# Seven arms by the token count, in steps of 16 rows, for the first products of the experts' second parts

## The chip, the cores and the metric

The kernel runs on one core of a Trainium2 chip. The metric is the device time of one execution in microseconds (us); for the kernel before, the median of three runs is 886.41 us.

## The reference

The reference chains three layers over 3072 tokens of 384 features: a gated linear attention, a mixture of eight experts in which every token goes to two, and a last feed-forward layer. The middle one is where the change lies:

```python
for e in range(E):
    for k in range(2):
        mask = top2[:, k] == e
        if not mask.any():
            continue
        h = np.maximum(x[mask] @ w1[e], 0.0)
        out[mask] += top2_w[mask, k, None] * (h @ w2[e])
```

`w1[e]` is 384 x 1024 and `w2[e]` 1024 x 384. How many tokens an expert gets follows from the inputs. Worked out from the reference's own inputs, the experts 0 to 7 get 766, 738, 811, 777, 800, 755, 719 and 778.

## The kernel before

The attention runs first, in 24 chunks of 128 tokens, and writes each token's features to two of 6656 slots: each of the eight experts (`NE`) owns 832 (`CAP`). [...] The first block holds 320, 384 or 512 slots and is always full; the second one holds the rest (512 for expert 0, 448 for experts 1 and 7, 320 for the others) and is only filled as far as the expert has tokens. Below, this block is called the expert's second part.

A step (`products`, one per block and per `f`, the eight groups of 128 hidden units) has two halves. The first products (`first_products`, line 218) are nine matmuls: weights split into two f16 parts times the tokens of the block, in three pieces of 128 features; their column count is the number of slots taken. The second products (`second_products`, line 237, and `tail_products`, line 269) take the hidden units of the step two steps back (`LAG`) and multiply them with `w2`, 128 slots at a time. `relu` (lines 244 and 252) runs between them on ACT and DVE, over the block's full width whatever the count.

`take_rows` loads the eight counts into registers of PE. For a second part, `either` (line 326) emits a binary tree of compares on the count: each leaf, called an arm here, is the same piece of code for one `cut`, the number of empty slots at the block's end that it leaves out. An arm of the first products is nine pairs of LDWEIGHTS and MATMUL and a jump to the end of the tree (the last arm needs no jump). The tail of the second products has a tree of its own. Before the change both trees use `CUTS` in steps of 32, four arms, or three where an expert's limit is 64. All arms stand in PE's program one behind the other, and the compares jump over those that aren't taken.

The order of the blocks is 0 to 2 with their first parts, then their second parts, then experts 3, 4 and 5 with both parts each, and at the end first parts of 6 and 7 and second parts of 6 and 7. One step of an expert's second part in the middle of its run is, in PE's program: a tree of the first products, three matmuls of the second products (nine for expert 0), and a tree of the tail, in whose arms three more matmuls and the tail's products stand. Second parts thus run, in the profile, for expert 0 near 187 to 217 us, 1 to 244 us, 2 to 268 us, 3 to 317 us, 4 to 367 us, 5 to 412 us and 6 and 7 to 506 us. The last feed-forward layer follows, without any branch on PE, and ends the kernel.

Of the kernel before, what the change touches and what calls it, by code (L numbers as in the profile page):

```python
# [30 lines left out]
def blocks(e):  # L31
    cut = {0: 320, 1: 384, NE - 1: 384}.get(e, 512)
    return (0, cut), (cut, CAP - cut)
# [4 lines left out]
CLEARED = 16  # L38
TAIL = 64
CUTS = (0, 32, 64, 96)  # L40


def parts(e, blk):
    n = blocks(e)[blk][1]
    return [(c, min(128, n - c)) for c in range(0, n, 128)]
# [32 lines left out]
def fast(ctx, tc, flag, f_cols, kq_cols, v_rows, gates, blank, void, w12, w_in, w_out, out):  # L78
# [126 lines left out]
    def lasting(e, blk, name, tag):  # L205
        if order.index((e, blk)) < 2:
            return bank(name, tag)
        if tag not in FIXED:
            FIXED[tag] = bank(name, tag)
        return FIXED[tag]  # L210

    def first_products(ph, n, lhs, key):
        x = XT[key]
        o = 0
        for a in range(3):
            wh, wl = lhs(a)
            for l, r in ((wh, a), (wh, 3 + a), (wl, a)):
                nc.tensor.matmul(ph[:, :n], l, x[:, r, :n], start=(o == 0), stop=(o == 8))  # L218
                o += 1

    def begin_second(key, f, parts):
        if f == 0:
            for i in range(len(parts)):
                new = bank if key[0] == "m" else partial(lasting, *key)
                PY[key, i] = new(f"py{i}", ("b0", "b1", "b5" if len(parts) == 3 else "b2", "b5")[i])[:, :DM]
        return HS.pop((key, f))

    def second_products(hs, key, f, last, rhs, parts):
        wh, wl = (w.rearrange("p a b -> p (a b)") for w in rhs)
        for i, (c0, m) in parts:  # L230
            p = PY[key, i]
            if m == 64:
                ops = [(hs[:, c0:c0 + 2 * m], w) for w in (wh, wl)]
            else:
                ops = [(hs[:, s + c0:s + c0 + m], w) for s, w in ((0, wh), (0, wl), (512, wh))]
            for o, (l, r) in enumerate(ops):
                nc.tensor.matmul(p[:max(m, 128)], l, r, start=(f == 0 and o == 0),  # L237
                                 stop=(f == last and o == len(ops) - 1))
# [17 lines left out]
    def tail_products(hs, e, f, rhs, cut):  # L256
        i, (c0, n) = list(enumerate(parts(e, 1)))[-1]
        p = PY[(e, 1), i].rearrange("p (a r) -> p a r", a=3)
        r = n - cut
        for a in range(3):  # L260
            wh, wl = (w[:, a, :] for w in rhs)
            if n == TAIL:
                both_halves = hs[:, c0:c0 + 2 * n].rearrange("p (h r) -> p h r", h=2)[:, :, :r]
                ops = [(p[:, a].rearrange("p (h r) -> p h r", h=2)[:, :, :r], wh, both_halves),
                       (p[:, a, :r], wl, hs[:, c0:c0 + r])]
            else:
                ops = [(p[:, a, :r], w, hs[:, at:at + r]) for w, at in ((wh, c0), (wl, c0), (wh, 512 + c0))]
            for o, (out_, l, x) in enumerate(ops):
                nc.tensor.matmul(out_, l, x, start=(f == 0 and a == 0 and o == 0),  # L269
                                 stop=(f == 7 and a == 2 and o == len(ops) - 1))  # L270
# [3 lines left out]
    def turn_tail(new):  # L274
        while turns:
            e, i, n, t = turns.pop(0)
            del PY[(e, 1), i]
            p = new("ph", next(tags["ph"]))[:, :DM]
            y = gath.tile([128, DM], F32, name="yo")
            if n == TAIL:  # L280
                nc.tensor.transpose(p[:, :128], t[:, :2 * n], ident)
                nc.tensor.transpose(p[:n, 128:256], t[:, 2 * n:3 * n], ident)
                nc.scalar.activation(y[:n, 128:256], p[n:2 * n, :128], AF.Copy)
                nc.vector.tensor_copy(y[:n].rearrange("p (a r) -> p a r", a=3)[:, 0:3:2],
                                      p[:n, :256].rearrange("p (a r) -> p a r", a=2))
            else:
                for a in range(3):
                    nc.tensor.transpose(p[:n, a * 128:(a + 1) * 128], t[:, a * n:(a + 1) * n], ident)
                nc.vector.tensor_copy(y[:n], p[:n])
            at = (e + 1) * CAP - n  # L290
            stores.append((y_rows[at:at + n, :], y[:n]))

    def results(e, blk):
        for i, (c, n) in enumerate(parts(e, blk)):
            p = PY[(e, blk), i]
            if blk and c + n == blocks(e)[1][1]:
                t = gath.tile([128, DM], F32, name="yo")
                if n == TAIL:
                    packed = t[:, :3 * n].rearrange("p (a r) -> p a r", a=3)
                    p = p.rearrange("p (a r) -> p a r", a=3)  # L300
                    nc.scalar.activation(packed, p[:, :, n:], AF.Copy)
                    nc.vector.tensor_tensor(packed, packed, p[:, :, :n], op=OP.add)
                else:
                    nc.scalar.activation(t, p, AF.Copy)
                turns.append((e, i, n, t))
                continue
            y = gath.tile([128, DM], F32, name="yo")
            PY.pop(((e, blk), i))
            if n == 64:
                nc.scalar.activation(y[:n], p[n:2 * n], AF.Copy)  # L310
                nc.vector.tensor_tensor(y[:n], y[:n], p[:n], op=OP.add)
            elif i % 2:
                nc.vector.tensor_copy(y[:n], p[:n])
            else:
                nc.scalar.activation(y[:n], p[:n], AF.Copy)  # L315
            at = e * CAP + blocks(e)[blk][0] + c
            stores.append((y_rows[at:at + n, :], y[:n]))
# [8 lines left out]
    def either(e, emit, cuts):  # L326
        if e is None or len(cuts) == 1:
            emit(cuts[0])
            return
        half = len(cuts) // 2  # L330
        with tc.If(many[e] > CAP - cuts[half]) as cond:
            either(e, emit, cuts[:half])
        with cond.Else():
            either(e, emit, cuts[half:])

    def products(first, second):
        if first:
            e, blk, f = first
            ph = lasting(e, blk, "ph", next(tags["ph"]))

            def emit_first(cut):
                w = RING[e, f]
                first_products(ph, blocks(e)[blk][1] - cut, lambda a: (w[:, 0, a, :], w[:, 1, a, :]), (e, blk))

        if second:
            e2, blk2, f2 = second
            hs = begin_second((e2, blk2), f2, parts(e2, blk2))

            w2 = RING[e2, f2]
            done = list(enumerate(parts(e2, blk2)))  # L350
            rhs = w2[:, 0, 3:6, :], w2[:, 1, 3:6, :]

            def emit_second(parts):
                second_products(hs, (e2, blk2), f2, 7, rhs, parts)

            def emit_tail(cut):
                emit_second(done[-2:-1])
                if cut < done[-1][1][1]:
                    tail_products(hs, e2, f2, rhs, cut)

        if first:
            either(e if blk else None, emit_first, CUTS[:3] if e in (1, 2) else CUTS)
        turn_tail(partial(lasting, NE - 1, 1))
        if second:
            if blk2:
                emit_second(done[:-2])
                either(e2, emit_tail, CUTS if done[-1][1][1] > TAIL else CUTS[:3])
            else:
                emit_second(done)
        if second and f2 == 7:  # L370
            results(e2, blk2)
        if first:
            relu(*first, ph)

    def moe_first(e, blk, f):
        products((e, blk, f), None)

    def moe_second(e, blk, f):
        products(None, (e, blk, f))
# [12 lines left out]
    def moe_products(n):  # L392
        products(moe_steps[n] if n < len(moe_steps) else None, moe_steps[n - LAG] if n >= LAG else None)
# [558 lines left out]
    for n in range(4, len(moe_steps) + LAG):  # L952
# [8 lines left out]
        e, blk, f = moe_steps[n]  # L961
# [143 lines left out]
    for n in range(M + FF_LAG):  # L1105
        if n < M:
            blk, f = steps[n]
# [317 lines left out]
```

## Time and profile before

| | |
|---|---|
| median of 3 runs | 886.41 us (886.34 to 888.34) |
| the profiled execution, own time | 889.56 us |
| its span | 887.8 us |
| PE busy with matmuls | 873.6 us, 98% |
| ACT / DVE / POOL busy | 600.6 / 575.0 / 172.3 us |
| chain that ended last | PE 91%, DMA 4%, the rest 1% each or less |
| PE's granted clock, mean over the span | 0.999 of full speed |

The span is the time from the first to the last instruction; 1.76 us of the profiled execution lie around it. Busy time of PE is a union of matmuls whose ends are modelled, so the pace of PE is read from the starts of groups that follow each other. PEq and PEld in the views are PE's sequencer, which reads the program, jumps, waits for semaphores and hands matmuls on, and its weight loads. A jump of either kind, with a condition or without, is a COMPARE_BRANCH of line 331 in the profile. Queue q8, "instruction", moves pieces of PE's program.

### The profile page before, as it was taken

How to read it: one execution, taken by the hardware profiler on the slowest of the kernel's cores; microseconds unless marked ns; L12 is line 12 of the kernel's file. 1: busy time of each engine (PE TensorE's matmuls, PEld its weight loads, DVE VectorE, ACT ScalarE, POOL GpSimd, SP SyncE). 2: the span in 40 equal slices, each digit the busy share in tenths (PEclk: the TensorE clock that was granted, in tenths of full speed). 3: DMA queues.
4: the chain of work that ended last, by engine and by line, in shares of the span. 5: the costliest groups of instructions: out<-in, count | busy, mean ns of one | idle time of the engine just before them, and what ended most of it. 6: DMA issues, size and time to landing. Idle time of an engine off the chain costs nothing.

```text
span 887.8 us, 18080 instructions
## 1 busy us (share of the span) xinstructions
PE 873.6 (98%) x6573; PEld 527.8 (59%) x6573; DVE 575.0 (65%) x1174; ACT 600.6 (68%) x1569; POOL 172.3 (19%) x240
## 2 busy tenths in 40 slices
PE   8999999999999999999999999999999999999996
PEld 7888766556665656566566555555555555555553
DVE  7998966733586565767658775565565565565664
ACT  7988855646786566778659776666657656656653
POOL 3488834100000000000004040130220320410000
PEclk9999999999999999999999999999999999999999
DMA  9989999844585665949366531030230220320101
GB/s 254 212 248 282 269 281 274 268 118 98 162 249 172 166 198 112 232 112 220 101 159 174 140 83 29 28 98 18 63 72 10 73 62 10 92 51 1 37 1 40
DMA packets 112343, 116.99 MB, mean 132 GB/s; under 512 B 68208, under 2 KB 91376, under 8 KB 112080
## 3 DMA queue, kind: packets, MB, share of 16 engines
q1 hardware_dynamic: 105792, 96.11, 41.5%
q0 software_dynamic: 6144, 18.88, 6.9%
q8 instruction: 77, 1.26, 0.6%
q14 instruction: 42, 0.34, 0.1%
q10 hardware_dynamic: 288, 0.39, 0.1%
HBM read 72.88 MB, written 30.38 MB: 116 GB/s over the span
## 4 chain that ended last, share of the span: by engine, by line
PE 91%; DMA 4%; POOL 1%; issue 1%; DVE 1%; ACT 1%; SPq 0%; POOLq 0%; DVEq 0%
PE ph L218 42%; PE py L237 41%; DMA kq<-in_kq_cols 2%; PE pY L562 2%; PE pA L539 1%; DMA raw<-in_w 1%; PE py L269 1%; PE pY L554 1%; DMA xt<-xs 1%; PE pkr L578 1%; PE pX L605 1%; DMA v<-in_v_rows 1%; POOL kqT L523 1%; POOL xs L707 1%; PE pt L625 0%
## 5 line engine op out<-in xcount | busy, mean ns | idle before, releaser
L237 PE MATMUL py<-wsplit,hs 128*128 128x384 f16 x2296 | 409.3, 326 | 0.0
L237 PEld LDWEIGHTS <-hs 128*128 128x128 f16 x2296 | 224.4, 98 | 157.7
L218 PE MATMUL ph<-xt,wsplit 128*128 128x512 f16 (+7 forms) x1152 | 211.9, 329 | 2.1 <-DMA xt<-xs 2.1
L218 PE MATMUL ph<-xt,winS 128*128 128x512 f16 x864 | 201.8, 379 | 0.0
L917 DVE SCALAR_TENSOR_TENSOR s<-s,z 128x512 f32<-128x512 f32 x96 | 66.5, 692 | 135.6 <-ACT s L914 135.6
L218 PEld LDWEIGHTS <-wsplit 128*128 128x128 f16 x1152 | 109.5, 98 | 75.0 <-issue 2.8
L913 ACT ACTIVATE z<-ph 128x512 f32<-128x512 f32 x96 | 57.3, 597 | 126.3 <-PE ph L218 126.3
L218 PEld LDWEIGHTS <-winS 128*128 128x128 f16 x864 | 84.4, 98 | 91.5
L252 DVE SCALAR_TENSOR_TENSOR hs<-ph,hs 128x256 f16<-128x256 f32 (+2 forms) x192 | 79.4, 441 | 75.4 <-ACT hs L244 73.2
L244 ACT ACTIVATE hs<-ph 128x512 f16<-128x512 f32 (+3 forms) x128 | 65.7, 513 | 72.7 <-PE ph L218 69.7
L159 DVE SCALAR_TENSOR_TENSOR wsplit<-raw,wsplit 128x768 f16<-128x768 f32 x72 | 68.8, 956 | 26.3 <-ACT wsplit L158 24.5
L164 ACT ACTIVATE junk<-wsplit 128x384 f16<-128x384 f16 x144 | 74.2, 516 | 1.5
L914 ACT ACTIVATE s<-z,bias_a 128x512 f32<-128x512 f32 x96 | 69.3, 722 | 3.1
L919 DVE SCALAR_TENSOR_TENSOR g<-s,ph 128x512 f32<-128x512 f32 x96 | 66.0, 687 | 6.1
L158 ACT ACTIVATE wsplit<-raw 128x768 f16<-128x768 f32 x72 | 60.1, 835 | 13.7 <-DMA raw<-in_w 10.9
L382 POOL CAST spacer<-hs 1x1 f32<-1x1 f16 x22 | 5.8, 262 | 327.5 <-ACT hs L244 326.9
L926 DVE TENSOR_TENSOR hs<-g,hs 128x512 f16<-128x512 f32 x96 | 65.7, 685 | 0.1
L382 POOL COPY spacer<-g 1x1 f32<-1x1 f32 x40 | 19.9, 497 | 215.7 <-DVE g L919 198.8
L925 ACT ACTIVATE hs<-g 128x512 f16<-128x512 f32 x96 | 58.8, 613 | 1.1 <-DVE g L919 1.1
L884 POOL DMA_INDIRECT g<-y_rows,yslot x48 | 50.9, 1061 | 20.9 <-issue 9.9
L707 POOL DMA_INDIRECT xs<-xkeep,yslot x48 | 49.1, 1023 | 15.7 <-issue 9.2
L315 ACT ACTIVATE yo<-py 128x384 f32<-128x384 f32 x26 | 12.8, 491 | 33.0 <-PE py L237 32.2
(163 smaller groups left out, 889.4 us busy)
## 6 DMA issues: line engine op xcount, KB each, us to landing
raw<-in_w SPq DMA_DIRECT2D x64, 384.0 KB
y_rows<-yo SPq DMA_DIRECT2D x48, 192.0 KB
kq<-in_kq_cols SPq DMA_DIRECT2D x42, 192.0 KB
w<-in_moe_w_out SPq DMA_DIRECT2D x32, 192.0 KB
w<-in_moe_w_in SPq DMA_DIRECT2D x24, 256.0 KB
v<-in_v_rows SPq DMA_DIRECT2D x24, 192.0 KB
out<-o SPq DMA_DIRECT2D x22, 192.0 KB
f<-in_f_cols SPq DMA_DIRECT2D x40, 96.0 KB
```

The source lines that it names most:

```text
L158: nc.scalar.activation(t[:, 0], raw, AF.Copy, scale=SW)
L159: nc.vector.scalar_tensor_tensor(t[:, 1], raw, SW, t[:, 0], op0=OP.mult, op1=OP.subtract)
L164: nc.scalar.activation(junk[:, :DM], RING[e, f][:, 0, 3 * i:3 * i + 3, :].rearrange("p a b -> p (a b)"), AF.Square, accum_out=wsum[:, 8 * ...
L218: nc.tensor.matmul(ph[:, :n], l, x[:, r, :n], start=(o == 0), stop=(o == 8))
L237: nc.tensor.matmul(p[:max(m, 128)], l, r, start=(f == 0 and o == 0), stop=(f == last and o == len(ops) - 1))
L244: nc.scalar.activation(hs[:, :n], ph[:, :n], AF.Relu, accum_out=hacc[:, at:at + 1])
L252: nc.vector.scalar_tensor_tensor(hs[:, at:at + hi - lo], ph[:, lo:hi], 0.0, hs[:, lo:hi], op0=OP.max, op1=OP.subtract)
L914: nc.scalar.activation(s, z, AF.Square, scale=1.0 / SZ, bias=bias_a)
L917: nc.vector.scalar_tensor_tensor(s, s, ZD, z, op0=OP.add, op1=OP.mult)
L919: nc.vector.scalar_tensor_tensor(g, s, 0.5, ph, op0=OP.mult, op1=OP.mult)
L925: nc.scalar.activation(hs[:, :512], g, AF.Copy)
L926: nc.vector.tensor_tensor(hs[:, 512:], g, hs[:, :512], op=OP.subtract)
```

## The change

A tuple of cuts in steps of 16 rows takes the place of `CUTS` in the tree of the first products alone: seven arms instead of four, and five instead of three for experts 1 and 2. The tree of the tail stays as it was.

```diff
 TAIL = 64
 CUTS = (0, 32, 64, 96)
+FINE = tuple(range(0, 97, 16))
...
         if first:
-            either(e if blk else None, emit_first, CUTS[:3] if e in (1, 2) else CUTS)
+            either(e if blk else None, emit_first, FINE[:5] if e in (1, 2) else FINE)
```

Two places in PE's program. The first is a step of expert 5's second part (`wsplit` are the weights, `xt` the tokens, `ph` the result; x2 marks two compares that follow each other). Before, from the tree's entry to the second products behind it:

```order
L331 COMPARE_AND_BRANCH x2
...
L218 MATMUL ph<-xt,wsplit 128x320
...
L218 MATMUL ph<-xt,wsplit 128x288
...
L331 COMPARE_AND_BRANCH
...
L218 MATMUL ph<-xt,wsplit 128x256
...
L218 MATMUL ph<-xt,wsplit 128x224
...
L237 LDWEIGHTS hs
```

and with the change, whose lines are one further down:

```order
L332 COMPARE_AND_BRANCH x2
...
L219 MATMUL ph<-xt,wsplit 128x320
...
L332 COMPARE_AND_BRANCH
...
L219 MATMUL ph<-xt,wsplit 128x304
...
L219 MATMUL ph<-xt,wsplit 128x288
...
L332 COMPARE_AND_BRANCH x2
...
L219 MATMUL ph<-xt,wsplit 128x272
...
L219 MATMUL ph<-xt,wsplit 128x256
...
L332 COMPARE_AND_BRANCH
...
L219 MATMUL ph<-xt,wsplit 128x240
...
L219 MATMUL ph<-xt,wsplit 128x224
...
L238 LDWEIGHTS hs
```

Three arms, of 304, 272 and 240 columns, and three compares are new; what comes behind the tree has moved 60 instructions further from its entry. The second place is a step of expert 2's second part. Before:

```order
L331 COMPARE_AND_BRANCH
L218 LDWEIGHTS wsplit
L218 MATMUL ph<-xt,wsplit 128x320
...
L331 UNCONDITIONAL_BRANCH
L331 COMPARE_AND_BRANCH
L218 LDWEIGHTS wsplit
L218 MATMUL ph<-xt,wsplit 128x288
```

and with the change:

```order
L332 COMPARE_AND_BRANCH x2
L219 LDWEIGHTS wsplit
L219 MATMUL ph<-xt,wsplit 128x320
...
L332 UNCONDITIONAL_BRANCH
L219 LDWEIGHTS wsplit
L219 MATMUL ph<-xt,wsplit 128x304
...
L332 UNCONDITIONAL_BRANCH
L332 COMPARE_AND_BRANCH
L219 LDWEIGHTS wsplit
L219 MATMUL ph<-xt,wsplit 128x288
```

A second compare stands at the entry and an arm of 304 columns has come in; further down one of 272 has too. On the other engines the instructions and their order are the same.

## Rows read from the trace of the kernel before

**Rows 1.** The page: span, PE's busy time, the queue of PE's program (packets, MB).

```profile
span 887.8 us, 18080 instructions
...
PE 873.6 (98%) x6573; PEld 527.8 (59%) x6573; DVE 575.0 (65%) x1174; ACT 600.6 (68%) x1569; POOL 172.3 (19%) x240
...
q8 instruction: 77, 1.26, 0.6%
```

**Rows 2.** Busy time by stretch (us; x instructions), PE's granted clock, in 395 to 410.

```profile
395.00:410.00 15.00, 15.00 (x109) 10.52 (x108) 11.83 (x36) 12.72 (x46) 0.00 (x0) 1.00 0.98 224
```

**Rows 3.** Groups of PE by shape, expert 7's: busy, mean ns | idle before.

```profile
L218 PE MATMUL ph<-xt,wsplit 128*128 128x416 f16 x72 | 14.0, 338 | 0.0
```

**Rows 4.** Timeline of PE (start us, us) in second parts of experts 0, 3, 5, 6, 7.

```profile
200.36 1.87 PE L218 MATMUL ph<-xt,wsplit 128*128 128x448 f16 x9
...
203.78 1.87 PE L218 MATMUL ph<-xt,wsplit 128*128 128x448 f16 x9
...
302.74 1.26 PE L218 MATMUL ph<-xt,wsplit 128*128 128x288 f16 x9
...
304.98 1.26 PE L218 MATMUL ph<-xt,wsplit 128*128 128x288 f16 x9
...
404.41 1.15 PE L218 MATMUL ph<-xt,wsplit 128*128 128x256 f16 x9
405.39 1.14 PE L237 MATMUL py<-wsplit,hs 128*128 128x384 f16 x6
406.37 1.15 PE L218 MATMUL ph<-xt,wsplit 128*128 128x256 f16 x9
407.35 1.14 PE L237 MATMUL py<-wsplit,hs 128*128 128x384 f16 x6
...
468.59 1.03 PE L218 MATMUL ph<-xt,wsplit 128*128 128x224 f16 x9
...
470.43 1.03 PE L218 MATMUL ph<-xt,wsplit 128*128 128x224 f16 x9
...
486.59 1.74 PE L218 MATMUL ph<-xt,wsplit 128*128 128x416 f16 x9
488.17 1.63 PE L237 MATMUL py<-wsplit,hs 128*128 128x384 f16 x9
...
489.80 1.74 PE L218 MATMUL ph<-xt,wsplit 128*128 128x416 f16 x9
```

**Rows 5.** All jumps of line 331: ns min/median/max, first and last start us.

```profile
L331 PEldq COMPARE_BRANCH  x328: 70/208/1868, 186.4 to 504.7; - x164
```

**Rows 6.** Six single long jumps of line 331, each in a window around its start.

```profile
L331 PEldq COMPARE_BRANCH  x1: 420/420/420, 401.5 to 401.5; - x1
L331 PEldq COMPARE_BRANCH  x1: 1868/1868/1868, 405.4 to 405.4; - x1
L331 PEldq COMPARE_BRANCH  x1: 417/417/417, 470.5 to 470.5; - x1
L331 PEldq COMPARE_BRANCH  x1: 630/630/630, 474.0 to 474.0; - x1
L331 PEldq COMPARE_BRANCH  x1: 348/348/348, 478.9 to 478.9; - x1
L331 PEldq COMPARE_BRANCH  x1: 1074/1074/1074, 481.4 to 481.4; - x1
```

**Rows 7.** Queue q8 in 403.20:403.30, 479.95:480.05, 470:484 (packets started, MB, share).

```profile
q8 instruction: 1, 0.02, 164.6%
q8 instruction: 1, 0.02, 68.2%
q8 instruction: 4, 0.07, 2.0%
```

**Rows 8.** Queue q8 in 565:590; busy by stretch between its two starts there.

```profile
q8 instruction: 2, 0.03, 0.6%
565.80:589.34 23.54, 23.54 (x129) 12.44 (x128) 14.36 (x23) 14.46 (x32) 9.40 (x12) 1.00 0.30 84
```

## The prediction

> **What bounds the kernel now.** The page comes first: PE is busy for 873.6 of 887.8 us [rows 1]. The timeline of PE then shows how tight that is: in second parts each group starts as the one before ends, and in 395 to 410 us PE is busy for 15.00 of 15.00 us at full granted clock [rows 2, 4]. So a column less on PE is time gained, and a gap on PE is time lost; nothing behind can make up for either, since the last layer is as full (23.54 of 23.54 us) [rows 8]. The third view is that of the sequencer's jumps, and the fourth the queue that brings PE's program. They show what keeps PE fed, and there I find the larger term.
>
> **What the change saves.** The arms follow from the counts. Expert 2 has 811 tokens, 21 slots empty: its cut goes from 0 to 16. Expert 3 (777, 55 empty) and expert 7 (778, 54 empty) go from 32 to 48. Expert 0 (66 empty), 4 (32), 5 (77) and 6 (113) stay at 64, 32, 64 and 96, and expert 1 (94) at its limit of 64. The trace bears the counts out where it can: expert 7 runs 72 matmuls of 416 columns [rows 3]. Nine products of 416 columns take 488.17 - 486.59 = 1.58 us, nine of 256 take 405.39 - 404.41 = 0.98 us [rows 4]: 3.75 ns a column. 16 columns over 8 steps are 0.48 us an expert, for three experts **1.44 us**, all on PE's path. `relu` works on the full width as before.
>
> **What it adds: compares.** Each of the 64 second-part steps runs one compare more. A jump takes 208 ns in the median and 70 at least [rows 5], so 64 cost the sequencer at most some 13 us, 0.2 us a step. I cost them at nothing by themselves: the 328 jumps of before leave PE without a gap, because the sequencer hands matmuls on well ahead. How far ahead can be read at expert 5. The jump that begins at 405.4 [rows 6] belongs to the tree of the tail, between the third and the fourth of the six second products that start at 407.35 [rows 4]; the fourth is due at 407.35 + 0.49 = 407.84. So the sequencer had 2.4 us in hand. That is the cover, and it is gone once the sequencer is late by more.
>
> **What it adds: code.** In the middle steps of experts 3 to 6 PE's program holds 78 instructions for the first products (four arms of 18, three jumps, three compares), 6 for three second products and 46 for the tail's tree, 130 in all. Three more arms with a jump each (57) and three compares make it 190. Counted alike, expert 0 goes from 192 to 252 a step, 7 from 136 to 196, 1 from 116 to 156 and 2 from 110 to 150. This program comes in pieces: 77 packets of 16.4 KB [rows 1], and from one start to the next PE runs 129 + 128 = 257 instructions where nothing is jumped over [rows 8]. Code that is jumped over is brought too: 4 packets start in 470 to 484 us [rows 7], some 1,000 instructions for about eight steps, of which some 35 each are run.
>
> **Is a piece ever late?** Yes, already now. A fetch started at 403.2 to 403.3 and took 164.6% x 16 x 0.1 us = 2.63 us, so it landed by 405.9 [rows 7]; the jump that began at 405.4 lasted 1.87 us and ended at 407.3 [rows 6], 1.4 us after the landing. The fetch of 480.0 took 1.09 us and landed at 481.1; the jump of 481.4 ended at 482.5, again 1.4 us later. Both waited for the newest piece, so only about one piece is brought ahead. The price of a piece is then the time from the end of one such jump to the end of the next. In experts 6 and 7 these ends are 470.9, 474.6, 479.2 and 482.5 [rows 6]: periods of 3.7, 4.6 and 3.3 us, mean **3.87 us**. Before, a piece of expert 6 holds 257/130 = 2.0 steps of 1.84 us (468.59 to 470.43 [rows 4]), 3.6 us of work: supply and demand just meet, and the 2.4 us in hand absorb the rest.
>
> **The sum.** With the change a piece holds less work: for expert 0, with steps of 3.42 us, 3.42 x 257/252 = 3.49 us; for 3 and 4 (2.24 us) 3.03; for 5 (1.96 us) 2.65; for 6 (1.84 us) 2.49; for 7 (3.21 us) 4.21 [rows 4]. Expert 4 runs the same shapes as 3. Experts 1 and 2 have more columns than 3, hence longer steps, and 156 and 150 instructions: at least 2.24 x 257/156 = 3.69, about even. Every piece that holds less than 3.87 us of work puts the sequencer back by the difference. Eight steps of 190 instructions are 5.9 pieces, six borders; the piece behind the first border was brought in the quiet steps before, so I count five waits, and seven for expert 0. Each second part starts with the 2.4 us in hand. PE then stands still for
>
> - expert 0: 7 x 0.38 - 2.4 = 0.3 us
> - experts 3 and 4: 5 x 0.84 - 2.4 = 1.8 us each
> - expert 5: 5 x 1.22 - 2.4 = 3.7 us
> - expert 6: 5 x 1.38 - 2.4 = 4.5 us
>
> together 12.1 us. Less 1.44 us that is **+10.7 us**. The profiled execution took 889.56 us (887.8 of span and 1.76 around it) and would take 900.3; it lies 3.15 us above the median of the runs, so I put the sum on the median: 886.41 + 10.7 = **897.1 us**.
>
> The unknown price is that of a piece, and both bounds come from the same rows. With the shortest period, 3.3 us, only experts 5 and 6 lose, 0.9 + 1.7 us: +1.1 us, 887.5. With the period of expert 5 as a fourth one, from the end of the jump of 401.5 (401.9) to that of 405.4 (407.3), 5.4 us, the mean is 4.25: experts 0, 3, 4, 5 and 6 lose 2.9, 3.7, 3.7, 5.6 and 6.4 us, +20.9, 907.3. I take the mean of the three since expert 6, where they lie, carries most of the loss; the 5.4 holds one fetch of 2.63 us, in a stretch with the DMA engines 98% busy [rows 2].
>
> [...] The rows show waits that end 1.4 us after the newest fetch has landed [rows 6, 7]. [...]
>
> **The rivals.**
>
> - *Not slower: the pieces come faster when they are asked for faster.* The period of 3.87 us is near the 3.6 us that PE's own pace demanded there, so part of it may be demand and not supply. Then the 2.4 us hold: expert 6 stays hidden with a period under 2.49 + 2.4/5 = 2.97 us, which is the point that decides. Only the gain is left: 885.0 us, within 0.3%. Against it: 1.4 us from landing to going on, 1.1 us of transfer (2.0% x 16 x 14 us over four [rows 7]), and a new fetch begins only after the last wait, which already is 2.5 us before any queueing of the fetch. Chance 0.12. [...]
> - *Hardly slower: the short period rules.* 3.3 us each time, 887.5 us, below what a measurement tells apart. For it: one of three periods; against it: the two others and expert 5's. Chance 0.10.
> - *Much slower: the fetch queues behind the weight loads.* As in 5.4 us above, in more than one piece in four: beyond 907 us. For it the 2.63 us of that fetch, against it the 1.1 us mean of four others. Chance 0.10.
> - *The finer arms aren't taken.* The counts are of the reference's own inputs, and the six other block widths fit them; the most that could be missing is the 1.44 us. It only shifts the others.
>
> **How the numbers follow.** The forecast, pieces of 3.4 to 4.25 us, gets 0.68, and its time is 897.1 us. The range reaches from the short period to the long mean, 887 to 907 us: it leaves out the first rival and what lies beyond 907, about 0.2. A measurement of this kernel tells about 0.3% from no change, 2.7 us, that is 883.8 to 889.1. Slower by more: forecast and third rival, 0.78. Within: the first two rivals, 0.20. Faster by more would need twice the gain that the columns hold: 0.02.
>
> **What the profile after would show.** 72 matmuls each of 304, 272 and 400 columns in place of 72 of 320, 288 and 416; nine of 400 columns in 1.52 us. 392 jumps instead of 328, and some 91 packets on q8 (48 x 60 + 16 x 40 = 3,520 more instructions are 13.7 pieces). Jumps over 1 us not twice but at most borders in experts 3 to 6, about 4 us apart; and gaps of about 1 us on PE there that no semaphore ends, before lines 219 and 238. The last layer keeps its length. Wrong it would be if PE stays without gaps in experts 5 and 6, or if gaps come that another engine ends.

## The result, and the profile after

The changed kernel takes 899.0 us in the median of six runs (896.98 to 904.54); six runs of the kernel before give 888.0 us. The ratio is 1.0133, with a 95% interval of 1.0110 to 1.0157: some 11.8 us slower, where 10.7 us (1.012) were forecast. The profiled execution took 896.98 us, the lowest of the six.

Its page, in the lines that answer to [rows 1], and PE's costliest group with its idle time:

```profile
span 895.2 us, 18144 instructions
...
PE 875.1 (98%) x6573; PEld 527.2 (59%) x6573; DVE 576.0 (64%) x1174; ACT 599.9 (67%) x1569; POOL 171.9 (19%) x240
...
q8 instruction: 91, 1.49, 0.7%
...
L219 PE MATMUL ph<-xt,wsplit 128*128 128x512 f16 (+9 forms) x1152 | 211.3, 329 | 7.0 <-issue 5.4
```

The same group before:

```profile
L218 PE MATMUL ph<-xt,wsplit 128*128 128x512 f16 (+7 forms) x1152 | 211.9, 329 | 2.1 <-DMA xt<-xs 2.1
```

The same 6573 matmuls run, 14 more packets come on q8, and PE has begun to wait in its first products for "issue", that is for nothing that the profile shows. The jumps, to be read against [rows 5]:

```profile
L332 PEldq COMPARE_BRANCH  x392: 65/208/2962, 183.5 to 512.9; - x196
```

There are 64 more, as many as there are steps, and the longest has gone from 1.87 to 2.96 us. Sixteen of them last over 1 us, where three did before: the two that the prediction names and a third one at 361.7 us, of 1.10 us. The forms of the first products show that the change does what it says:

```profile
L219 PE MATMUL ph<-xt,wsplit 128*128 128x400 f16 x72 | 13.5, 332 | 0.0
...
L219 PE MATMUL ph<-xt,wsplit 128*128 128x304 f16 x72 | 10.6, 293 | 0.2 <-issue 0.2
...
L219 PE MATMUL ph<-xt,wsplit 128*128 128x272 f16 x72 | 9.6, 279 | 0.8 <-issue 0.8
```

Where the time went is read by stretch: each second part from its first product to that of the next block. The columns are length, then PE's busy time and count, PEld, DVE, ACT, POOL, granted clock, DMA share and GB/s. Before, experts 2 to 7 and the sum of all eight stretches were

```profile
241.70:262.20 20.50, 20.50 (x165) 13.98 (x163) 16.62 (x44) 17.59 (x56) 0.00 (x0) 1.00 0.91 250
292.20:311.70 19.50, 19.50 (x169) 13.83 (x168) 11.04 (x35) 11.87 (x45) 0.00 (x0) 1.00 0.64 171
341.40:361.00 19.60, 19.60 (x171) 13.89 (x169) 11.73 (x36) 12.33 (x46) 0.00 (x0) 1.00 0.67 171
390.70:408.30 17.60, 17.60 (x134) 12.92 (x132) 13.21 (x38) 13.71 (x50) 0.00 (x0) 1.00 0.70 175
462.10:477.80 15.70, 15.70 (x129) 12.20 (x127) 11.17 (x34) 11.91 (x44) 4.17 (x8) 1.00 0.61 140
477.80:505.90 28.10, 28.06 (x208) 16.72 (x207) 23.49 (x54) 23.02 (x62) 5.68 (x9) 1.00 0.64 160
sum 173.10, PE 173.06 PEld 114.77 DVE 109.77 ACT 126.10 POOL 9.85; mean PE 21.63 PEld 14.35 DVE 13.72 ACT 15.76 POOL 1.23
```

and after:

```profile
238.80:260.90 22.10, 20.60 (x167) 13.98 (x165) 17.06 (x44) 18.54 (x57) 0.00 (x0) 1.00 1.06 253
290.80:311.20 20.40, 19.57 (x170) 13.92 (x169) 11.06 (x35) 11.90 (x45) 0.00 (x0) 1.00 0.76 178
340.90:360.60 19.70, 19.70 (x169) 13.90 (x167) 11.68 (x36) 12.27 (x46) 0.00 (x0) 1.00 0.67 135
390.40:412.10 21.70, 19.55 (x134) 13.42 (x133) 13.32 (x38) 13.70 (x50) 0.00 (x0) 0.92 0.83 197
465.90:484.80 18.90, 16.35 (x128) 11.83 (x126) 12.35 (x37) 13.17 (x48) 4.88 (x9) 1.00 0.56 137
484.80:513.50 28.70, 27.70 (x209) 16.72 (x207) 22.30 (x51) 21.68 (x57) 5.02 (x8) 1.00 0.63 145
sum 183.60, PE 175.56 PEld 114.97 DVE 110.28 ACT 126.91 POOL 9.90; mean PE 21.95 PEld 14.37 DVE 13.78 ACT 15.86 POOL 1.24
```

The second parts have grown by 183.60 - 173.10 = 10.5 us; PE, busy for all of them before, now stands still for 183.60 - 175.56 = 8.0 us there. The two profiled executions differ by 7.4 us only, because what lies ahead (the attention and the first parts of experts 0 to 2) happened to end 2.9 us earlier in the later one (the first product of expert 0's second part starts at 186.7 instead of 189.6 us); the last layer took 381.7 us instead of 381.9.

The longest wait, in expert 5, in the timeline of PE:

```profile
402.21 1.16 PE L219 MATMUL ph<-xt,wsplit 128*128 128x256 f16 x9
403.20 1.14 PE L238 MATMUL py<-wsplit,hs 128*128 128x384 f16 x6
406.49 1.55 PE L219 MATMUL ph<-xt,wsplit 128*128 128x256 f16 x9 [2.15 <-issue]
407.83 2.13 PE L238 MATMUL py<-wsplit,hs 128*128 128x384 f16 x6
409.75 1.53 PE L219 MATMUL ph<-xt,wsplit 128*128 128x256 f16 x9
411.12 1.14 PE L238 MATMUL py<-wsplit,hs 128*128 128x384 f16 x6
```

The single jump in it, and the fetch of q8 that starts in 403.75 to 403.85:

```profile
L332 PEldq COMPARE_BRANCH  x1: 2962/2962/2962, 403.5 to 403.5; - x1
```

```profile
q8 instruction: 1, 0.02, 81.2%
```

The fetch took 81.2% x 16 x 0.1 = 1.30 us and landed at 405.1. The jump, begun at 403.5, ended at 406.4, 1.4 us after the landing, and the matmuls start at 406.49. It is the same wait as the 1.87 us of [rows 6], but now the matmuls in hand had run out at 404.3. All sixteen jumps over 1 us end so, 1.2 to 1.5 us after the newest fetch on q8 has landed.

### The profile page after: what moved, and what is told of

The parts are those of the page before. It is cut to its first block, busy times and chain, and to the rows that moved or that the text cites. A ratio compares the mean times of both kernels' runs of the same rounds, so it can differ in the third digit from the quotient of the medians.

```text
span 895.2 us, 18144 instructions
## 1 busy us (share of the span) xinstructions
PE 875.1 (98%) x6573; PEld 527.2 (59%) x6573; DVE 576.0 (64%) x1174; ACT 599.9 (67%) x1569; POOL 171.9 (19%) x240
## 5 line engine op out<-in xcount | busy, mean ns | idle before, releaser
L219 PE MATMUL ph<-xt,wsplit 128*128 128x512 f16 (+9 forms) x1152 | 211.3, 329 | 7.0 <-issue 5.4
```

## The experiments

Theory A is that of the prediction: pieces of PE's program come too late for code that is longer but holds no more work. Theory B is that the compares themselves cost the time. Each ratio is to runs of the kernel before that were taken together with the experiment: 889.11 us in the median for the first four experiments, 887.18 us for the last four.

**The code alone.** An arm that no expert takes (for expert 2 another one than for the rest) gets a tree and copies of its own; cuts and compares on the path stay as before. In the diffs `blk` is 0 for an expert's first part and 1 for its second.

```diff
+            spare = 2 if e == 2 else 0
+            more = range(3 if e in (1, 2) else 4)
+
+            def emit_padded(i):
+                cut = CUTS[i // 32]
+                if blk and cut == CUTS[spare]:
+                    either(e, lambda _: emit_first(cut), [CAP - 5000 - c for c in more])
+                else:
+                    emit_first(cut)
...
-            either(e if blk else None, emit_first, CUTS[:3] if e in (1, 2) else CUTS)
+            either(e if blk else None, emit_padded, CUTS[:3] if e in (1, 2) else CUTS)
```

> The kernel before, with the added code but neither the finer cuts nor a compare more on the path: in one arm that no expert takes (cut 0; for expert 2, which takes that one, cut 64) stand four copies of the arm behind a tree of its own (three copies for experts 1 and 2). Theory A (pieces of PE's program come too late): some 91 packets on q8, 328 jumps run, no column fewer, and PE stands still in second parts of experts 3 to 6 as forecast for the change, 12.1 us: 1.0136 times the kernel before, no less than 1.008. Theory B (the added compares cost the time, the code does not): the time of before, 0.997 to 1.003.

Measured: 1.0175 (1.0157 to 1.0193), 904.18 us against 889.11. Its jumps, its q8 and the sum of its eight second parts:

```profile
L331 PEldq COMPARE_BRANCH  x328: 70/197/2842, 184.5 to 514.6; - x164
```

```profile
q8 instruction: 91, 1.49, 0.7%
```

```profile
sum 185.50, PE 175.25 PEld 114.30 DVE 113.20 ACT 128.09 POOL 9.81; mean PE 21.91 PEld 14.29 DVE 14.15 ACT 16.01 POOL 1.23
```

Code that never runs makes the kernel slower, with no compare more on the path: B falls. It costs 15.6 us by the ratio, against 13.2 of the change with its gain of 1.44 added back, though the intervals of the two overlap; the forecast of 1.0136 (12.1 us) lies below this one. The second parts grew by 185.50 - 173.10 = 12.4 us in the profile, which is the fastest of the five runs (899.79 us). All 13 jumps over 1 us in it end 1.4 to 1.6 us after the newest fetch has landed.

**A compare alone.** One compare more on the path of each step, over two instructions and a jump.

```diff
+            def tree():
+                either(e if blk else None, emit_first, CUTS[:3] if e in (1, 2) else CUTS)
+
+            if blk:
+                with tc.If(many[e] > 5000) as cond:
+                    w = RING[e, f]
+                    nc.tensor.matmul(ph[:, :64], w[:, 0, 0, :], XT[e, blk][:, 0, :64], start=True, stop=True)
+                with cond.Else():
+                    tree()
+            else:
+                tree()
...
-            either(e if blk else None, emit_first, CUTS[:3] if e in (1, 2) else CUTS)
```

> The kernel before with one compare more on the path of each of the 64 second-part steps, and hardly more code: ahead of the tree of the first products stands a compare that never holds, over one LDWEIGHTS, one MATMUL and a jump (four instructions a step). Theory A: 392 jumps are run as in the changed kernel, but a piece still holds 257/134 x 1.84 = 3.5 us of work in expert 6, five waits of 0.3 us stay within the 2.4 us in hand, and the time is that of before, 0.997 to 1.003. Theory B (the compares): 64 x 0.2 us, up to 13 us, 1.012 to 1.015.

Measured: 1.0018 (1.0005 to 1.0032). Inside A's range and far from the 1.012 of B. In its profile the second parts sum to 173.4 us, where 173.1 stood before. The small rest (1.6 us) fits the four instructions a step and the 0.2 us less in hand, but no run parts the two.

**Seven arms for experts 5 and 6 alone.**

```diff
-            either(e if blk else None, emit_first, FINE[:5] if e in (1, 2) else FINE)
+            either(e if blk else None, emit_first, FINE if e in (5, 6) else CUTS[:3] if e in (1, 2) else CUTS)
```

> The seven arms for experts 5 and 6 alone, which take no other cut by them; the others keep four or three. Theory A: 3.7 + 4.5 = 8.2 us slower, 1.009 (1.005 to 1.014), with all long waits in these two second parts. Theory B: 16 of the 64 compares, a quarter of the 12 us: 3 us, 1.0035.

Measured: 1.0096 (1.0070 to 1.0123). B's 1.0035 is excluded. Two of eight experts, those with the shortest steps and no column to gain, cost 8.5 us, about two thirds of the 13.2 us (11.8 and the 1.44) that the change costs before its gain. In its profile the second parts of 5 and 6 last 24.0 and 19.4 us instead of 17.6 and 15.7, while those of 3 and 4 keep 19.6 each, and all five jumps over 1 us stand in 5 and 6.

**Finer arms for experts 2 and 7 alone.**

```diff
-            either(e if blk else None, emit_first, FINE[:5] if e in (1, 2) else FINE)
+            either(e if blk else None, emit_first, FINE if e == 7 else FINE[:5] if e == 2 else CUTS[:3] if e == 1 else CUTS)
```

> The finer arms for experts 2 (five) and 7 (seven) alone; both take a cut of 16 rows more and their steps are long, so that a piece holds about 3.9 and 4.2 us of work. Theory A: the gain without the loss, 2 x 0.48 = 0.96 us faster, 0.999 (0.996 to 1.002), no wait that reaches PE. Theory B: 16 compares, 3 us less 0.96: 1.002 or more.

Measured: 1.0013 (1.0002 to 1.0024), inside A's range, but the gain of 0.96 us isn't there, and B's 1.002 lies inside the interval too: this run doesn't part the two. In its profile these second parts hold two gaps, together more than the 0.96. One of 0.57 us in expert 2 is put down to the weights' split on DVE, which ended 0.2 us before PE went on; it also ended 1.3 us after a fetch had landed (at 259.7 us), so late code is neither shown nor excluded there. The other, 0.55 us in expert 7, is put down to the `yo` of DVE, and nearly the same (0.53 us) stands in the kernel with the columns alone below, which adds no code. What took the gain stays open.

**Six arms**, as a dose between four and seven.

```diff
-            either(e if blk else None, emit_first, CUTS[:3] if e in (1, 2) else CUTS)
+            either(e if blk else None, emit_first, CUTS[:3] if e in (1, 2) else (0, 16, 32, 48, 64, 96))
```

> Six arms (0, 16, 32, 48, 64, 96) for experts 0 and 3 to 7, three as before for 1 and 2: a dose between four and seven. 170 instructions a step in experts 3 to 6. Theory A: a piece holds 3.39 us of work in experts 3 and 4, 2.96 in 5 and 2.78 in 6, with one border less: experts 5 and 6 lose 4 x 0.91 - 2.4 = 1.2 and 4 x 1.09 - 2.4 = 2.0 us, the others nothing; experts 3 and 7 gain 0.96 us. +2.3 us, 1.0025 (0.999 to 1.007). If the loss went with the added code in proportion (two thirds of it for most experts): +7 us, 1.008.

Measured: 1.0054 (1.0034 to 1.0073). Inside A's range and less than in proportion to the code (1.008), as a cover that must first be used up has it, but twice the sum's 1.0025. In its profile, the slowest of its six runs, expert 5 grew by 4.3 us, where 1.2 were forecast, and expert 6 by 2.2, where 2.0 were. One jump in expert 5 lasted 4.18 us. The sum takes every piece at the mean price; that single dear ones make up the difference is what this one profile suggests, not more.

**Steps of 8 rows**, the change taken further.

```diff
-FINE = tuple(range(0, 97, 16))
+FINE = tuple(range(0, 97, 8))
...
-            either(e if blk else None, emit_first, FINE[:5] if e in (1, 2) else FINE)
+            either(e if blk else None, emit_first, FINE[:9] if e in (1, 2) else FINE)
```

> The change taken further: steps of 8 rows, thirteen arms (nine for experts 1 and 2), 310 instructions a step in experts 3 to 6. Columns: expert 5 gains 8 rows more, 1.7 us in all. Theory A: now every second part is short of code and the time is that of its pieces. With 3.87 us a piece: expert 0 10.6 waits of 1.5 us, 1 next to nothing, 2 6.2 of 1.1, 3 and 4 8.65 of 2.0 each, 5 8.65 of 2.25, 6 8.65 of 2.34, 7 8.8 of 1.3, less 2.4 each: +90 us, 1.10 (1.06 with 3.3 us a piece, 1.13 with 4.25). The mean period between pieces can be read directly there. Theory B (compares): one more level than seven arms, 128 compares in all over before: +25 us at most, 1.03. If a piece came faster when asked for faster (2.5 us): under 1.03 too.

Measured: 1.1040 (1.1003 to 1.1077), 978.19 us. Experts 0, 1, 2, 5 and 6 by stretch, and q8 in expert 6's stretch:

```profile
187.20:223.50 36.30, 29.10 (x207) 16.38 (x205) 12.26 (x29) 18.91 (x63) 0.00 (x0) 1.00 0.39 78
223.50:252.00 28.50, 25.48 (x165) 14.49 (x166) 11.26 (x34) 17.95 (x61) 0.00 (x0) 1.00 0.50 134
252.00:283.50 31.50, 22.60 (x165) 14.39 (x166) 16.08 (x39) 16.71 (x53) 0.00 (x0) 0.95 0.73 181
438.40:471.70 33.30, 21.21 (x133) 12.56 (x132) 15.23 (x43) 15.01 (x54) 0.00 (x0) 0.90 0.53 131
525.50:556.40 30.90, 20.26 (x127) 12.80 (x126) 13.01 (x38) 14.05 (x51) 5.01 (x9) 0.87 0.35 86
```

```profile
q8 instruction: 9, 0.15, 2.1%
```

PE has work for 15.7 us in expert 6's second part, its length before, and takes 30.9 for it. Nine fetches start in this stretch, the first at 526.6 and the last at 554.6 us, so a piece comes every 28.0/8 = 3.5 us. Read alike, it comes every 3.8 us in expert 3 and every 3.9 us in 4 and 5; over the four the mean is 3.76 us. This is the price of a piece where it alone sets the pace, and it refutes the rival by which pieces come faster when asked for faster, which needed less than 2.97. All 51 jumps over 1 us in this profile end 1.3 to 1.7 us after the newest fetch has landed.

The sum came out right (about 91 us against 90), but its terms didn't. Experts 3 to 6 together grew by 57.2 us instead of 64.7 and expert 0 by 8.4 instead of 13.5; expert 1, put at next to nothing, grew by 4.3, and experts 2 and 7 by 22.2 instead of 13.4. These errors cancel, which is luck. PE's granted clock, 0.87 and 0.90 in experts 6 and 5, was lower, which the sum had not; what that adds isn't parted here.

**The columns alone.** As many arms as before, cuts that fit these counts.

```diff
-            either(e if blk else None, emit_first, CUTS[:3] if e in (1, 2) else CUTS)
+            fits = {2: (0, 16, 64), 3: (0, 48, 64, 96), 7: (0, 48, 64, 96)}
+            either(e if blk else None, emit_first, fits.get(e, CUTS[:3] if e == 1 else CUTS))
```

> As many arms as before, with cuts that fit the counts: 0, 16, 64 for expert 2 and 0, 48, 64, 96 for 3 and 7. The columns of the changed kernel without its code. Theory A: the whole gain, 1.44 us, 0.9984 (0.996 to 1.0005), no gap on PE in second parts; nine products of 400 columns in 1.52 us.

Measured: 0.9987 (0.9974 to 1.0000), 886.5 us against 887.18. The forecast gain of 1.44 us (0.9984) is inside the interval, and so, just, is none. It has the lowest ratio of all versions tried, but its cuts are chosen for these inputs. Its profile holds the narrow products without a gap before them, and as many packets on q8 as before. Against what was expected, expert 7's second part has a gap: PE waits 0.53 us there until the `yo` of DVE. The products and the packets:

```profile
L218 PE MATMUL ph<-xt,wsplit 128*128 128x400 f16 x72 | 13.5, 332 | 0.0
...
L218 PE MATMUL ph<-xt,wsplit 128*128 128x304 f16 x72 | 10.6, 293 | 0.0
...
L218 PE MATMUL ph<-xt,wsplit 128*128 128x272 f16 x72 | 9.6, 279 | 0.0
```

```profile
q8 instruction: 77, 1.26, 0.6%
```

**One far jump.** 792 instructions that aren't run, at one place.

```diff
+            def emit_far(cut):
+                for _ in range(45 if (e, blk, f, cut) == (3, 1, 4, 0) else 1):
+                    emit_first(cut)
...
-            either(e if blk else None, emit_first, CUTS[:3] if e in (1, 2) else CUTS)
+            either(e if blk else None, emit_far, CUTS[:3] if e in (1, 2) else CUTS)
```

> The kernel before with one long piece of code that isn't run: in one step alone (expert 3, second part, f = 4) the arm that isn't taken holds its nine products 45 times, 792 instructions more, 3.1 pieces. Theory A, pieces brought one after the other whatever is jumped over: the jump there lasts three periods, some 11 us, PE stands still for 9 us at that place, q8 has 80 packets, 1.010. Theory A', a jump has its target's piece brought at once: one period, 1 to 2 us of standing still, q8 has 77 or 78 packets, 1.001 to 1.003.

Measured: 1.0080 (1.0056 to 1.0103), between the two. The jump alone, the packets that start while it lasts (297.7 to 302.8 us), and PE's timeline around it:

```profile
L331 PEldq COMPARE_BRANCH  x1: 4979/4979/4979, 297.7 to 297.7; - x1
```

```profile
q8 instruction: 2, 0.03, 2.6%
```

```profile
299.05 0.32 PE L269 MATMUL py<-hs,wsplit 128*128 128x64 f16 x6
302.78 2.34 PE L218 MATMUL ph<-xt,wsplit 128*128 128x288 f16 x9 [3.41 <-issue]
304.91 2.13 PE L237 MATMUL py<-wsplit,hs 128*128 128x384 f16 x6
```

The jump takes 4.98 us, until 302.7; three periods would be some 11. Two fetches start while it lasts, at 298.5 and 300.3 us, and it ends 1.3 us after the second has landed. The whole run has 79 packets, two more than before for 3.1 pieces of code. Both fit a jump that leaves out a piece lying wholly between, but which pieces came isn't shown. PE stands still for 3.4 us and then runs at half its pace: nine products in 2.13 us (302.78 to 304.91) instead of 1.10 (296.98 to 298.08 in the same timeline). The two steps from 302.78 to 309.97 take 7.19 us instead of 4.48, so the slow pace costs 2.7 us more. Together they are 6.1 of the 7.1 us that the ratio gives.

## Why the prediction was right

**What bounds.** Right: second parts without a gap before have grown by 10.5 us, and nothing behind them made up for it.

**The columns.** 1.44 us forecast. Nine products of 400 columns take 1.52 us in the changed kernel, from 493.16 to 494.68 in its timeline, where those of 416 took 1.58 [rows 4]; the kernel with the columns alone gained 0.0013 x 887.2 = 1.2 us by its ratio, with an interval that holds 1.44.

**The compares at nothing.** Right: the compare alone costs 1.6 us, 2.8 at the upper end of its interval, and it brings four instructions a step with it.

**The code.** Right as mechanism: code that never runs makes the kernel slower (1.0175), and the long jumps end 1.2 to 1.6 us after a fetch has landed, in the changed kernel and with the code alone, where [rows 6, 7] had 1.4 us. The size, 12.1 us before the gain, is near the change's 13.2 and below the 15.6 of the code alone. By expert, in us, loss less gain as forecast against the growth between the two profiled executions, and the growth with the code alone, which has no gain in it:

| expert | 0 | 1 | 2 | 3 | 4 | 5 | 6 | 7 | sum |
|---|---|---|---|---|---|---|---|---|---|
| forecast for the change | 0.3 | 0 | -0.5 | 1.3 | 1.8 | 3.7 | 4.5 | -0.5 | 10.7 |
| the change | 0 | 0 | 1.6 | 0.9 | 0.1 | 4.1 | 3.2 | 0.6 | 10.5 |
| the code alone | 0 | 0.1 | 0.3 | 3.2 | 1.7 | 3.8 | 3.0 | 0.3 | 12.4 |

The sum is better than its terms, and in this it had luck. Before their gain the changed kernel's second parts lost 12.0 us in the profile, against 12.1 forecast; but 3.2 of them lie in experts 2 and 7, which were put at nothing, and 1.7 are lost in expert 5 to a lower clock (0.50 in 407.83 to 409.75 us), which the sum didn't have (below). The waits in experts 3 to 6 took the remaining 7.1 us, where 11.8 were forecast.

Expert 2, put at "about even", lost 2.1 us before its gain. Gaps of 0.52 and 0.20 us before 255.2 us are put down to "issue". Then one jump lasted 2.74 us, from 256.8 to 259.6, and ended 1.5 us after its fetch had landed. The profile puts the gap that ends with it, 0.75 us, down to the `hs` of ACT, though PE's sequencer was still in that jump when ACT had done. Expert 7 lost 1.1 us before its gain, 1.0 of it in two gaps of 0.56 and 0.44 us at its end (up to 511.24 and 512.18 us). The profile puts them down to the `hs` of ACT and DVE, which end within 0.1 us before PE goes on; gaps that another engine ends were named as a sign of being wrong, and here there are some. Expert 7's second part varies without any code of its own, too: 28.1 us before, 28.8 with the columns alone, 29.9 with the far jump, whose code lies in expert 3. So this loss isn't shown to be one of code. Expert 4 lost next to nothing, and why isn't shown. Expert 6 lost 3.2 instead of 4.5: five fetches start in its stretch, where six borders were counted, and its long jumps end at 471.3, 475.1, 478.8 and 482.4 us, 3.7 us apart instead of 3.87. Where a dear piece falls differs from run to run: with the same code, expert 5 grew by 4.1 us in the profile of the change and by 6.4 in that of seven arms for experts 5 and 6 alone. The times of the changed kernel differ too, 896.98 to 904.54 us.

**The price of a piece.** 3.87 us taken from three periods; 3.76 us in the mean of four experts where fetching alone sets the pace (steps of 8 rows), 3.5 in one of them. This term was right to 3%. What the sum had wrong is how many pieces come late and where.

**The rivals.** Pieces that come faster when asked: no, by the steps of 8 rows and by the code alone. The short period alone: no, the change costs 11.8 us and not 1.1. The much slower one: no. That the added code costs nothing, with PE's next piece there in time: no, by the code alone (1.0175), whose long jumps end 1.4 to 1.6 us after the newest piece has landed. No run shows how many pieces PE holds.

## What to carry to other kernels

An arm that was never taken wasn't free (1.0175 with the code alone): here PE's program came in pieces of 257 instructions at 3.5 to 3.9 us each, jumped-over code of such arms included, so a loop step with many arms needed as much work per piece as that. Before adding arms to such a kernel, count the instructions a step holds, taken or not, work out how long PE is busy with 257 of them, and compare that with the period between the ends of long jumps (here 3.3 to 4.6 us before the change, in experts 6 and 7). In the kernel before, full PE together with a jump that ended 1.4 us after a fetch had landed [rows 6, 7] meant a reserve nearly used up: of the 2.4 us in hand some 0.5 were left. Columns can be saved without that price by moving cuts instead of adding them, though here the gain, 1.2 us, is just not clear of noise.

## What the runs showed that was not expected

**PE's clock fell after some gaps.** The granted clock of the changed kernel in 404 to 407, 407 to 411 and 411 to 415 us:

```profile
404.00:407.00 3.00, 0.85 (x8) 0.47 (x6) 1.99 (x6) 1.32 (x5) 0.00 (x0) 1.00 0.99 384
407.00:411.00 4.00, 4.00 (x20) 2.50 (x19) 0.98 (x3) 1.34 (x5) 0.00 (x0) 0.57 1.13 240
411.00:415.00 4.00, 4.00 (x24) 2.15 (x22) 2.08 (x7) 2.69 (x10) 0.00 (x0) 1.00 0.33 90
```

PE had stood still for 2.15 us; shortly after it began again the granted clock fell: it was 0.50 from 407.83 to 409.75, and the six second products that start at 407.83 took 1.92 us instead of 0.98. From 406.49 to 411.12 PE did in 4.63 us what takes 0.98 + 0.98 + 0.98 = 2.94 before: 1.7 us of expert 5's 4.1. After the far jump's gap of 3.41 us nine products took 2.13 us instead of 1.10, and the mean clock of that profiled run was 0.994 instead of 0.999; that the clock fell there too is an estimate from these numbers. After the gaps of 1.08 and 1.02 us in expert 6 (until 475.45 and 482.95) it stayed at 1.00. The length of the gap alone didn't decide it: with steps of 8 rows PE stood still for 2.21 us in expert 0, until 208.66, and the clock stayed at 1.00 in that whole stretch (its row above). What else did isn't shown.

**A jump over three pieces cost 5 us, not three times the price of a piece.** Two fetches start while it lasts, where the longest jump of [rows 6] had waited for a single fetch. What a jump over more pieces would cost wasn't tried.
